# An attention and two gated projections on one core: later conversions, fewer raw tiles in flight, a third v buffer, and no 224-column product

## The chip, the cores and the metric

One NeuronCore of a Trainium2 chip runs the whole kernel. TensorE (PE) multiplies, VectorE (DVE), ScalarE (ACT) and GpSimd (POOL) do the elementwise work, SyncE (SP) issues the DMAs. The metric is the device time of one execution in microseconds (us); lower is better.

## The reference, cut to what matters

```python
# q, k, v: (4, 8, 576, 64); attention with a mask of its own for each half of the heads
scores = scale * np.matmul(q, k.transpose(0, 1, 3, 2))
mask_local   = (rel >= 0) & (rel < 32)                       # heads 0 to 3
mask_strided = (rel >= 0) & (pos_k % 32 == pos_q % 32)       # heads 4 to 7
scores = np.where(masks, scores, -1e9) - max
attn = np.exp(scores); attn = attn / (sum + 1e-9)
x = np.matmul(attn, v)              # then (2304 tokens, 512)
h = x @ w_in;  x = (h * np.cos(h)) @ w_out                   # 512 -> 2048 -> 512
g = x @ w_gate; x = (g * sigmoid(g) * (x @ w_val)) @ w_out2  # 512 -> 1536 -> 512
```

The weights reach the chip as 64-bit floats, and each projection is computed from two f16 halves of each operand, with three products (high by high, high by low, low by high).

## The kernel before, in words

The order of all work is written out by hand; each engine takes its instructions in program order, and SP takes the DMA issues in program order.

**Attention.** A unit is one batch and one pair of heads (16 units), worked in pairs of a strided and a local unit. Each unit has three groups, so 48 groups, alternating strided and local; six groups make a pair of units. The loop over k runs over the groups with lags: at step k come the sums of group k-2, the transposes (PE) of group k-5, the scores of group k (f32 products of 64 by 64, then the mask added by a bf16 product with an identity), the row maxima (DVE), the copy to the output tile `xy` of group k-7 (`put`, ACT), the evacuation of the transposes of k-5 (ACT), the products with v of k-6, the exponentials of k-1 (ACT), then `pump`, then the normalization of k-2 (POOL). `scale_q` (POOL) scales the q of the next pair's units at the third and fourth group of a pair. Line 361, in `scores`, adds a product of 224 columns of ones in an unused part of the bank. PSUM has four banks for scores, and a new one waits until the exponentials of its former user are done. `keep_warm` is a product of 384 columns into a bank of its own; before the change it runs only behind group 47.

**Loads.** `load_qk` brings a unit's q and k (three buffers per kind), `load_v` its v (two buffers per kind: two DMAs for a strided unit, one for a local one). At the last group of a pair the q/k of the third next pair and the v of the next pair are issued. `load_raw` brings one 128 x 512 tile of weights in 64-bit words, in the order of `order`: 16 tiles of w_in, 16 of w_out (scanned for their maxima), again 16 of w_out and so on. `RAW` tiles are in flight; each conversion or scan issues the next.

**Conversions.** A list (`fill`) of small steps with a cost each (about us of DVE) runs beside the main work. `pump(share)` adds `share` to a credit and runs steps while the credit is positive. For w_in a tile costs 1.62: `g0` (ACT, cost 0, line 207, reads the raw tile), `g1`, `g2`, `g3` (DVE, lines 210, 214, 218); the `g0` of the next tile is emitted ahead of the `g1` of this one, and `g3` issues the next raw load. Before w_in's tile `XSAT` + 1 come the maxima and the split of block 0 of the tokens. Then come the splits of w_in into halves, each beside a scan of a w_out tile (1.33 together). `KP` is the first group at which the pump runs, `PUMP` its share.

**Projections.** Behind the attention the first projection runs over five blocks of tokens and 16 tiles of w_in, each with 12 products of 512 columns (lines 465 to 467), then ACT and DVE make the cosine (lines 496 to 507); w_out is converted and used from about the 23rd of these steps on, the other weights later. `need` runs the list up to a wanted step.

Of the kernel before, what the change touches and what calls it, by code (L numbers as in the profile page):

```python
# [10 lines left out]
F32 = mybir.dt.float32  # L11
# [18 lines left out]
LT = S // 64  # L30
LW = 64 + STRIDE
# [6 lines left out]
SP = -(-ST // 2)  # L38
# [9 lines left out]

LAGS = (2, 5, 6, 7)
WARM = 11  # L50
PUMP, KP = 1.0, 5
XSAT = 12
EARLY, K0 = 1, 1
HEAD = 21
RATE, MINLAG = 0.8, 2
RAW = 6
XM = 3
SHARE, SHARE2, SHARE3, SB = 0.95, 0.8, 0.4, 2

# [1 line left out]
def is_local(p):  # L61
    return p < NPAIR // 2
# [6 lines left out]
def build(tc, qk_l, qk_s, v_l, v_s, w_in, w_out, w_gate, w_val, w_out2, mask_l, mask_s, eye32, eye16, out):  # L69
    nc = tc.nc  # L70
    wide = w_in.dtype != F32
    with ExitStack() as ctx:
# [11 lines left out]
        id16 = small.tile([128, 128], BF16, name="id16")  # L84
        ones16 = small.tile([128, 128], BF16, name="ones16")
# [58 lines left out]
        def load_raw():  # L144
            if not order:
                return
            mat, i = order.popleft()
            src = MATS[mat][i]
            if wide:
                t = ring.tile([128, 512, 2], I32, name="raw", bufs=RAW)  # L150
                nc.sync.dma_start(out=t.rearrange("p n w -> p (n w)"), in_=src.bitcast(I32))
            else:
                t = ring.tile([128, 512], F32, name="raw", bufs=RAW)
                nc.sync.dma_start(out=t, in_=src)
            raw.setdefault((mat, i), deque()).append(t)
# [20 lines left out]
        def pump(share):  # L176

            credit[0] = min(credit[0] + share, max(share, 1.0))
            while fill and credit[0] > 0:
                step_fill()  # L180
# [114 lines left out]
        ap = attn.enter_context(tc.tile_pool(name="attn", bufs=2, side="right"))  # L295
        pm = ctx.enter_context(tc.tile_pool(name="pm", bufs=4, space=bass.MemoryType.PSUM))
        pa = attn.enter_context(tc.tile_pool(name="pa", bufs=2, space=bass.MemoryType.PSUM))
        id32 = ap.tile([128, 128], F32, name="id32", bufs=1)
        ml = ap.tile([128, 4, LW], BF16, name="ml", bufs=1)
        ms = ap.tile([128, 4, SW], BF16, name="ms", bufs=1)  # L300
        e_s = [ap.tile([128, 4, 64], F32, name=f"e_s{i}", bufs=1) for i in range(4)]
        e_l = [ap.tile([128, 3, LW + 1], F32, name=f"e_l{i}", bufs=1) for i in range(4)]
        hot = ap.tile([128, 512], BF16, name="hot", bufs=1)
        nc.vector.memset(hot, 1.0)
        v_pair = [ap.tile([128, 2 * SP, 128], F32, name=f"v_pair{i}", bufs=1) for i in range(2)]
        for d in e_s:
            nc.gpsimd.memset(d, 0.0)
            nc.gpsimd.memset(d[:, :, SW:SW + 1], 1e-9)
# [5 lines left out]
        units = [(b, p) for b in range(NB) for p in (2, 0, 3, 1)]  # L314
        qk_t, v_t = {}, {}

        def load_qk(i):
            b, p = units[i]
            loc = is_local(p)
            qk_t[i] = ap.tile([128, QKW[loc]], F32, name="qkl" if loc else "qks", bufs=3)  # L320
            nc.sync.dma_start(out=qk_t[i], in_=(qk_l if loc else qk_s)[b, p % 2])

        def load_v(i):
            b, p = units[i]
            loc = is_local(p)
            if loc:
                v_t[i] = ap.tile([LW, LT, 128], F32, name="vl")
                nc.sync.dma_start(out=v_t[i], in_=v_l[b, p % 2])
            else:
                v_t[i] = v_pair[i // 2 % 2]  # L330
                for u in range(2):
                    nc.sync.dma_start(out=v_t[i][64 * u:64 * u + SW, SP * u:SP * u + SP, :], in_=v_s[b, p % 2, u])

# [7 lines left out]
        class Group:  # L341
# [7 lines left out]
            def scores(self):  # L349
                n, w = self.n, self.w  # L350
                b = bank()
                self.sc = b[:, 0:n * w].rearrange("p (n w) -> p n w", w=w)
                mask = (ml[:, 0:3] if self.g == 0 else ml[:, 1:4]) if self.loc else ms[:, 0:n]
                for i in range(n):
                    q0 = (64 if self.loc else SW) * (self.i0 + i)
                    k0 = (S if self.loc else QP) + q0
                    for h in range(2):
                        r = slice(64 * h, 64 * h + 64)
                        nc.tensor.matmul(out=self.sc[r, i, :], lhsT=qk_t[self.i][r, q0:q0 + 64], rhs=qk_t[self.i][r, k0:k0 + w],  # L359
                                         start=i == 0, stop=False)  # L360
                nc.tensor.matmul(out=b[:, 288:512], lhsT=ones16, rhs=hot[:, 0:224], start=False, stop=False)  # L361
                nc.tensor.matmul(out=self.sc, lhsT=id16, rhs=mask, start=False, stop=True)

            def top(self):
# [188 lines left out]
        gs = [Group(i + d, g) for i in range(0, len(units), 2) for g in range(3) for d in range(2)]  # L553
        load_qk(0)
        load_qk(1)
        for t, a in ((id16, eye16), (ms, mask_s), (ml, mask_l), (id32, eye32)):
            nc.sync.dma_start(out=t, in_=a)
        load_v(0)
        load_v(1)
        load_raw()  # L560
        load_qk(2)
        load_raw()
        load_qk(3)
        load_raw()
        load_v(2)
        load_v(3)
        load_raw()
        load_qk(4)
        load_raw()
        load_qk(5)  # L570
        load_raw()
        warm = bank()
        for _ in range(WARM):
# [14 lines left out]
        def keep_warm():  # L588
            t = bank()[:, 0:4 * LW].rearrange("p (n w) -> p n w", w=LW)
            nc.tensor.matmul(out=t, lhsT=id16, rhs=ml, start=True, stop=True)  # L590

        for k in range(len(gs) + LAGS[3] + 1):
            def group(lag):
                return gs[k - lag] if 0 <= k - lag < len(gs) else None
            i, g = 2 * (k // 6), k % 6
            if group(LAGS[0]):
                group(LAGS[0]).sums()
            if group(LAGS[1]):
                group(LAGS[1]).transposes()
            if group(0):  # L600
                group(0).scores()
                group(0).top()
                if g in (2, 3) and i + g < len(units):
                    scale_q(i + g)
            begun = k - len(gs) - K0
            if 0 <= begun < 2 * EARLY:
                m = begun // 2
                if begun % 2 == 0:
                    need(("in", m))
                    early = up1(0, m, range(KC // 2))  # L610
                else:
                    up1(0, m, range(KC // 2, KC), early)
                    up1_a(early)
                    steps.append((0, m, early))
                    if m:
                        up1_b(steps[-2][2])
            elif not group(0):
                keep_warm()
            if group(LAGS[3]):
                group(LAGS[3]).put()  # L620
            if group(LAGS[1]):
                group(LAGS[1]).evac()
            if group(LAGS[2]):
                group(LAGS[2]).values()
            if group(0) and g == 5:
                for j in (i + 6, i + 7):
                    if j < len(units):
                        load_qk(j)
                for j in (i + 2, i + 3):
                    if i and j < len(units):  # L630
                        load_v(j)
            if group(1):
                group(1).exps()
            pump(PUMP if k >= KP else 0)
            if group(LAGS[0]):
                group(LAGS[0]).norm()

# [213 lines left out]
```

## Time and profile before

| | |
|---|---|
| median of 3 runs | 947.25 us (943.33 to 947.49) |
| profiled execution | 946.87 us, span of its trace 944.9 us |
| PE busy | 909.9 us (96% of the span) |
| DVE busy | 505.2 us (53%) |
| ACT busy | 410.3 us (43%) |
| POOL busy | 130.7 us (14%) |
| mean granted clock of TensorE | 0.98 |
| DMA | 72.12 MB, mean 76 GB/s |

The profiled execution stands 2.0 us above its own span, and 0.4 us below the median. The shares are averages over stages with different limits: the attention takes the first 112 us, the first projection with its cosine the time up to about 520 us, the gated one the rest.

### The profile page before, as it was taken

To read this page: it belongs to the slowest core of one execution; us is meant where nothing else is said; L and a number is where in the kernel's file an instruction comes from. 1 tells how busy PE (TensorE), PEld (TensorE's weight loads), DVE (VectorE), ACT (ScalarE), POOL (GpSimd) and SP (SyncE) were. 2 spreads that over 40 slices of the span, in tenths; PEclk is the share of its full clock that TensorE was granted. 3 is DMA by queue.
4 is the path that set the end of the run, shared out by engine and by line. 5 is a ranking of instruction groups with operands and counts; after the bars stand their busy time and mean duration, and the time that the engine had idled before them with its cause. 6 is when DMAs were issued, how large, how long until landed. Compare 5 with 4: busy or idle time off the path is not lost.

```text
span 944.9 us, 14190 instructions
## 1 busy us (share of the span) xinstructions
PE 909.9 (96%) x5608; PEld 474.5 (50%) x5608; DVE 505.2 (53%) x1012; ACT 410.3 (43%) x845; POOL 130.7 (14%) x175
## 2 busy tenths in 40 slices
PE   7999978799999998999999999999999999999998
PEld 4667633344444443444577544444444444444587
DVE  4599877879833557693375663333233322332333
ACT  4689977765432445754465432222112211221222
POOL 3244223221121021222222000000000000000000
PEclk7599999999999999999999999999999999999999
DMA  9998841246400222051000200010001000100010
GB/s 305 309 298 256 261 132 45 89 136 192 142 0 23 90 90 67 1 222 45 23 23 24 67 1 1 1 44 1 1 1 45 1 1 0 45 1 1 8 38 23
DMA packets 21554, 72.12 MB, mean 76 GB/s; under 512 B 2704, under 2 KB 3472, under 8 KB 21488
## 3 DMA queue, kind: packets, MB, share of 16 engines
q1 hardware_dynamic: 21488, 71.22, 23.6%
q8 instruction: 44, 0.72, 0.3%
q14 instruction: 22, 0.18, 0.1%
HBM read 66.49 MB, written 4.72 MB: 75 GB/s over the span
## 4 chain that ended last, share of the span: by engine, by line
PE 80%; DVE 9%; ACT 6%; issue 3%; POOL 1%; DMA 1%; SPq 0%; ACTq 0%; DVEq 0%; POOLq 0%
PE bank L465 13%; PE bank L466 13%; PE bank L467 13%; PE acc L466 10%; PE acc L467 10%; PE acc L465 10%; PE bank L359 3%; PE po L412 3%; DVE tb L505 1%; PE tp L390 1%; DVE cv L218 1%; DVE tb L499 1%; PE bank L361 1%; PE tp L394 1%; ACT wo L228 1%
## 5 line engine op out<-in xcount | busy, mean ns | idle before, releaser
L465 PE MATMUL bank<-xs,spare 128*128 128x512 f16 (+1 forms) x480 | 171.9, 358 | 0.3 <-DVE ta L535 0.3
L466 PE MATMUL bank<-xs,spare 128*128 128x512 f16 (+1 forms) x480 | 171.9, 358 | 0.0
L467 PE MATMUL bank<-xs,spare 128*128 128x512 f16 (+1 forms) x480 | 171.9, 358 | 0.0
L465 PE MATMUL bank<-xs,wi 128*128 128x512 f16 (+1 forms) x320 | 115.9, 362 | 19.0 <-DVE tb L505 15.3
L535 DVE SCALAR_TENSOR_TENSOR ta<-ta,bank 128x512 f32<-128x512 f32 (+1 forms) x60 | 38.1, 635 | 168.9 <-ACT ta L534 168.9
L466 PE MATMUL bank<-xs,wi 128*128 128x512 f16 (+1 forms) x320 | 116.0, 362 | 0.0
L467 PE MATMUL bank<-xs,wi 128*128 128x512 f16 (+1 forms) x320 | 115.8, 362 | 0.0
L534 ACT ACTIVATE ta<-bank,c 128x512 f32<-128x512 f32 (+1 forms) x60 | 38.6, 643 | 168.6 <-PE bank L467 168.6
L466 PEld LDWEIGHTS <-wi 128*128 128x128 f16 x560 | 54.9, 98 | 76.4 <-issue 25.1
L537 ACT ACTIVATE g<-ta 128x512 f16<-128x512 f32 (+1 forms) x60 | 35.3, 588 | 132.5 <-DVE ta L536 132.5
L496 ACT ACTIVATE tb<-bank,quarter,c 128x512 int32<-128x512 f32 (+1 forms) x80 | 58.3, 729 | 70.2 <-PE bank L467 54.1
L466 PE MATMUL acc<-g,wi 128*128 128x512 f16 (+1 forms) x240 | 85.9, 358 | 0.9 <-DVE g L538 0.6
L465 PE MATMUL acc<-g,wi 128*128 128x512 f16 (+1 forms) x240 | 85.9, 358 | 0.4 <-ACT g L537 0.4
L467 PE MATMUL acc<-g,wi 128*128 128x512 f16 (+1 forms) x240 | 86.0, 358 | 0.0
L465 PEld LDWEIGHTS <-wi 128*128 128x128 f16 x560 | 55.0, 98 | 59.7 <-issue 6.3
L467 PEld LDWEIGHTS <-wi 128*128 128x128 f16 x560 | 55.0, 98 | 56.8 <-issue 3.8
L507 POOL TENSOR_TENSOR g<-tb,g 128x512 f16<-128x512 f32 (+1 forms) x48 | 50.8, 1059 | 186.7 <-ACT g L506 163.1
L466 PEld LDWEIGHTS <-spare 128*128 128x128 f16 x480 | 46.9, 98 | 46.8 <-issue 0.6
L465 PEld LDWEIGHTS <-spare 128*128 128x128 f16 x480 | 46.9, 98 | 46.5
L467 PEld LDWEIGHTS <-spare 128*128 128x128 f16 x480 | 46.9, 98 | 46.5
L501 ACT ACTIVATE tb<-tb,right 128x512 f32<-128x512 f32 (+1 forms) x80 | 53.9, 674 | 36.7 <-DVE tb L499 36.2
L467 PE MATMUL acc<-g,wo 128*128 128x512 f16 (+1 forms) x192 | 66.0, 344 | 0.0
(122 smaller groups left out, 1445.5 us busy)
## 6 DMA issues: line engine op xcount, KB each, us to landing
raw<-w_out SPq DMA_DIRECT2D x56, 512.0 KB, 5.3
raw<-w_in SPq DMA_DIRECT2D x16, 512.0 KB
raw<-w_gate SPq DMA_DIRECT2D x12, 512.0 KB, 3.8
raw<-w_val SPq DMA_DIRECT2D x12, 512.0 KB, 4.6
qks<-qk_s SPq DMA_DIRECT2D x8, 594.0 KB, 5.2
qkl<-qk_l SPq DMA_DIRECT2D x8, 592.0 KB, 8.6
out<-xy SPq DMA_DIRECT2D x16, 256.0 KB, 2.3
vl<-v_l SPq DMA_DIRECT2D x8, 432.0 KB, 6.7
```

What stands on the lines that cost most here:

```text
L218: nc.vector.scalar_tensor_tensor(out=u, in0=box["l"], scalar=29, in1=u, op0=ALU.logical_shift_right, op1=ALU.bitwise_or)
L359: nc.tensor.matmul(out=self.sc[r, i, :], lhsT=qk_t[self.i][r, q0:q0 + 64], rhs=qk_t[self.i][r, k0:k0 + w], start=i == 0, stop=False)
L412: nc.tensor.matmul(out=self.po[64 * h:64 * h + 64, i * qn:i * qn + qn], lhsT=v_t[self.i][0:r, t, 64 * h:64 * h + 64], rhs=pt[:, 64 * h:64 ...
L465: nc.tensor.matmul(out=o, lhsT=w[:, 0, c], rhs=x[0], start=first, stop=False)
L466: nc.tensor.matmul(out=o, lhsT=w[:, 0, c], rhs=x[1], start=False, stop=False)
L467: nc.tensor.matmul(out=o, lhsT=w[:, 1, c], rhs=x[0], start=False, stop=last)
L496: nc.scalar.activation(out=c["w"].bitcast(I32), in_=c["ph"], func=AF.Identity, scale=turn[c["blk"]], bias=quarter)
L501: nc.scalar.activation(out=c["w"], in_=c["w"], func=AF.Sin, scale=TWO_PI, bias=right)
L507: nc.gpsimd.tensor_tensor(out=g[:, 1, 0:n], in0=w, in1=g[:, 0, 0:n], op=ALU.subtract)
L534: nc.scalar.activation(out=t, in_=pg, func=AF.Tanh, scale=half[blk])
L535: nc.vector.scalar_tensor_tensor(out=t, in0=t, scalar=1.0, in1=pg, op0=ALU.add, op1=ALU.mult)
L537: nc.scalar.activation(out=g[:, 0, 0:n], in_=t, func=AF.Copy)
```

## The change

The pump starts at group 7 instead of 5 and adds 0.85 instead of 1.0; the scaling of block 0 comes after tile 10 instead of 12. Three raw tiles are loaded at the start, a fourth is added at group 24, and there are four buffers instead of six. v has three buffers of each kind, and its loads move from the last group of a pair to the first of the next. The first loads come in another order: q/k 0 and 1, the masks and the bf16 identity, q/k 2 and 3, the f32 identity, v 0 to 3, then raw tiles between q/k 4 and 5. The 224-column product of each group is taken out, and `keep_warm` runs at groups 3 to 8.

```diff
-PUMP, KP = 1.0, 5
-XSAT = 12
+PUMP, KP = 0.85, 7
+XSAT = 10
-RAW = 6
+RAW = 4
...
-        v_pair = [ap.tile([128, 2 * SP, 128], F32, name=f"v_pair{i}", bufs=1) for i in range(2)]
+        v_pair = [ap.tile([128, 2 * SP, 128], F32, name=f"v_pair{i}", bufs=1) for i in range(3)]
...
-                v_t[i] = ap.tile([LW, LT, 128], F32, name="vl")
+                v_t[i] = ap.tile([LW, LT, 128], F32, name="vl", bufs=3)
...
-                v_t[i] = v_pair[i // 2 % 2]
+                v_t[i] = v_pair[i // 2 % 3]
...
-                nc.tensor.matmul(out=b[:, 288:512], lhsT=ones16, rhs=hot[:, 0:224], start=False, stop=False)
...
-        for t, a in ((id16, eye16), (ms, mask_s), (ml, mask_l), (id32, eye32)):
+        for t, a in ((ms, mask_s), (ml, mask_l), (id16, eye16)):
             nc.sync.dma_start(out=t, in_=a)
-        load_v(0)
-        load_v(1)
-        load_raw()
         load_qk(2)
-        load_raw()
         load_qk(3)
-        load_raw()
-        load_v(2)
-        load_v(3)
+        nc.sync.dma_start(out=id32, in_=eye32)
+        for i in range(4):
+            load_v(i)
         load_raw()
         load_qk(4)
+        load_qk(5)
         load_raw()
-        load_qk(5)
         load_raw()
...
+            if 3 <= k < 9:
+                keep_warm()
...
+            if group(0) and g == 0:
+                for j in (i + 2, i + 3):
+                    if i and j < len(units):
+                        load_v(j)
             if group(0) and g == 5:
                 for j in (i + 6, i + 7):
                     if j < len(units):
                         load_qk(j)
-                for j in (i + 2, i + 3):
-                    if i and j < len(units):
-                        load_v(j)
...
             pump(PUMP if k >= KP else 0)
+            if k == len(gs) // 2:
+                load_raw()
```

## Rows read from the trace of the kernel before

**Rows 1.** The page's head and slices: the span in 40 equal parts of 23.6 us. Digits are busy tenths, PEclk is the granted clock in tenths of full speed, GB/s what the DMA engines moved.

```profile
span 944.9 us, 14190 instructions
PE   7999978799999998999999999999999999999998
PEclk7599999999999999999999999999999999999999
DMA  9998841246400222051000200010001000100010
GB/s 305 309 298 256 261 132 45 89 136 192 142 0 23 90 90 67 1 222 45 23 23 24 67 1 1 1 44 1 1 1 45 1 1 0 45 1 1 8 38 23
```

**Rows 2.** Windows by stage: from and to, length, busy time (and instructions) of PE, PE's weight loads, DVE, ACT and POOL, then the granted clock, the DMA engines' share, GB/s.

```profile
0.00:106.00 106.00, 99.79 (x1392) 68.67 (x1394) 80.43 (x226) 79.27 (x292) 39.01 (x82) 0.86 0.91 288
112.00:260.00 148.00, 131.59 (x640) 59.27 (x639) 119.25 (x208) 99.66 (x162) 34.87 (x33) 0.99 0.42 129
600.00:700.00 100.00, 100.00 (x465) 45.24 (x463) 32.56 (x52) 20.93 (x33) 0.00 (x0) 1.00 0.03 11
```

**Rows 3.** The chain of waits in order of time, 0 to 300 us, of it the score products of groups 7, 13, 15, 17 and 47 (local groups, 12 products each): start, length, what.

```profile
21.47 1.15 PE bank L359 x12
...
40.53 1.15 PE bank L359 x12
...
45.91 0.64 PE bank L359 x12
49.45 0.64 PE bank L359 x12
...
105.95 0.64 PE bank L359 x12
```

**Rows 4.** The timeline from 10 to 19 us: start, length, engine, line, operation, out<-in, count, and in brackets the idle time before it and what ended it. The first four lines are groups 4, 0 and 2; the last is the scores of group 6.

```profile
10.24 0.43 PEld L359 LDWEIGHTS bank<-qks 64*64 64x64 f32 x12 [0.21 <-ACT e_s L373]
10.84 0.23 PE L362 MATMUL bank<-ms,id 128*128 128x162 bf16 x1
10.88 0.17 DVE L382 RECIPROCAL ls<-ls 128x4 f32<-128x4 f32 x1
11.05 0.90 ACT L373 ACTIVATE e_s<-bank,mx 128x54 f32<-128x54 f32 x4 [0.19 <-DVE ls L382]
13.36 0.69 POOL L339 TENSOR_SCALAR qks<-qks 128x594 f32<-128x594 f32 x1 [6.57 <-DMA qks<-qk_s]
14.01 0.55 POOL L383 TENSOR_TENSOR e_s<-e_s,ls 128x216 f32<-128x216 f32 x1
14.61 0.29 PEld L394 LDWEIGHTS tp<-id,e_s 128*128 128x128 f32 x2 [3.77 <-POOL e_s L383]
18.23 1.10 PE L359 MATMUL bank<-qks 64*64 64x54 f32 x16
```

**Rows 5.** Windows of 0.1 and 0.2 us around the fall and the rise of the granted clock (third number from the end).

```profile
13.20:13.40 0.20, 0.00 (x0) 0.00 (x0) 0.00 (x1) 0.00 (x0) 0.04 (x1) 1.00 1.04 419
13.40:13.60 0.20, 0.00 (x0) 0.00 (x0) 0.00 (x0) 0.00 (x0) 0.20 (x1) 0.67 1.10 435
...
44.00:44.10 0.10, 0.10 (x6) 0.10 (x6) 0.00 (x1) 0.10 (x1) 0.10 (x1) 0.50 0.79 179
44.20:44.40 0.20, 0.20 (x12) 0.20 (x11) 0.00 (x0) 0.20 (x2) 0.20 (x1) 1.00 0.86 228
```

**Rows 6.** The timeline of PE: the 224-column product (L361) and the product behind it (L362) at the low and at the full clock, and two keep-warm products (L590) with what follows them.

```profile
35.10 0.37 PE L361 MATMUL bank<-hot,ones 128*128 128x224 bf16 x1
35.27 0.45 PE L362 MATMUL bank<-ml,id 128*128 128x288 bf16 x1
...
84.21 0.27 PE L361 MATMUL bank<-hot,ones 128*128 128x224 bf16 x1
84.32 0.29 PE L362 MATMUL bank<-ml,id 128*128 128x288 bf16 x1
...
116.43 0.50 PE L590 MATMUL bank<-ml,id 128*128 128x384 bf16 x2
116.76 0.38 PE L465 MATMUL bank<-xs,wi 128*128 128x512 f16 x1
```

**Rows 7.** Windows of 10 us, columns as in rows 2.

```profile
0.00:10.00 10.00, 8.35 (x74) 4.18 (x75) 4.26 (x8) 2.01 (x5) 3.34 (x24) 1.00 0.81 250
10.00:20.00 10.00, 6.03 (x58) 3.68 (x59) 5.27 (x17) 6.21 (x22) 3.64 (x6) 0.67 1.03 341
20.00:30.00 10.00, 10.00 (x105) 6.93 (x105) 5.11 (x15) 6.08 (x22) 3.07 (x6) 0.50 1.02 389
...
90.00:100.00 10.00, 10.00 (x169) 7.13 (x168) 9.39 (x30) 9.71 (x38) 4.83 (x8) 1.00 0.73 241
```

**Rows 8.** DMA issues: out<-in, engine, operation, count, size of one, median us from issue to landing where the trace has it.

```profile
raw<-w_in SPq DMA_DIRECT2D x16, 512.0 KB
...
qks<-qk_s SPq DMA_DIRECT2D x8, 594.0 KB, 5.2
...
vl<-v_l SPq DMA_DIRECT2D x8, 432.0 KB, 6.7
v_pair<-v_s SPq DMA_DIRECT2D x16, 162.0 KB
```

**Rows 9.** Waits, who for whom: us in total, times, the longest. The first is of all engines from 112 to 260 us (the same total stands for 0 to 260), the second of SP's queue from 0 to 130 us.

```profile
PE bank L465 <- DVE tb L505: 15.3, 9, 4.8
...
SPq L151 <- DVE wi L218: 40.2, 12, 7.5
```

**Rows 10.** The timeline from 16 to 19 us: the first conversion of a raw tile, its four instructions (the ACT line holds those of two tiles).

```profile
16.18 1.24 ACT L207 ACTIVATE wi<-raw 128x512 f32<-128x512 f32 x2
...
17.41 0.68 DVE L210 TENSOR_REDUCE pw_in<-raw 128x1 f32<-128x512 f32 x1
18.00 0.42 DVE L214 TENSOR_SCALAR wi<-wi 128x512 int32<-128x512 int32 x1
18.45 0.69 DVE L218 SCALAR_TENSOR_TENSOR wi<-raw,wi 128x512 int32<-128x512 int32 x1
```

**Rows 11.** The timeline of PE at 157 us, in the first projection.

```profile
157.08 0.38 PE L465 MATMUL bank<-xs,wi 128*128 128x512 f16 x1 [1.81 <-DVE tb L505]
```

## Prediction

> **What bounds the kernel now.** I read the page's slices first. TensorE (PE) is at 9 tenths of nearly every slice, so whatever moves the end must move PE; but its granted clock is 0.5 in the second slice, and the DMA engines are at 8 or 9 tenths through the first four slices and idle later [rows 1]. Then the windows by stage. The attention (0 to 106 us) has PE busy 99.8 of 106 us at a mean clock of 0.86 and the DMA at 0.91. From 112 to 260 us PE is busy only 131.6 of 148 us; later it is full [rows 2]. All that the diff touches lies in the first 112 us, with an echo up to 260 us. So the sum goes over when the attention ends, and over whether the stage behind it waits more.
>
> Then the chain of waits in order of time. The scores of group 7 start at 21.47, of group 13 at 40.53, of group 15 at 45.91, of group 17 at 49.45, of group 47 at 105.95 us [rows 3]. From 7 to 13 a group takes 19.06 / 6 = 3.18 us, from 17 to 47 it takes 56.5 / 30 = 1.883 us. The narrow windows say why: the granted clock falls to 0.5 (1.2 GHz) at 13.5 us and is back at 1.0 (2.4 GHz) at 44.2 us [rows 5], although PE had no gap for most of that time. What PE did before the fall stands in the timeline: its next weight load stood at 14.61 after 3.77 us of waiting for GpSimd (POOL), whose normalization of group 0 started at 14.01. Its operand was ready at 11.05, but ahead of it in POOL's queue stood the scaling of the third q/k tile, which waited 6.57 us for a DMA, up to 13.36 [rows 4]. So a late load stops POOL, POOL stops PE, PE loses its clock, and nine groups (6 to 14) run at 3.18 us.
>
> **The change part by part.** *New order of loads.* The q/k tiles 2 and 3 are now issued ahead of all v and raw tiles. A q/k tile is 594 KB (0.61 MB), a v pair 162 x 2 + 432 KB (0.77 MB), a raw tile 512 KB (0.52 MB) [rows 8]; masks and identities are 0.25 MB by their shapes. The queue moved 250 GB/s in the first 10 us, 341 in the next, 389 in the third [rows 7]: 2.5 MB by 10 us, 5.9 by 20, 9.8 by 30. In the order of before tile 2 ends at 3.37 MB, which this rate puts at 12.6 us, and it landed at 13.36: about 0.8 us is to be added. In the new order it ends at 2.0 MB, so it lands by 9 us. Then group 0 is normalized at 11.05 to 11.6 us, and its transposes go at about 12.8 instead of 14.61. In between, the new keep-warm products each take one of the four PSUM banks, so the scores of groups 3 and 4 wait for ScalarE's (ACT) exponentials of groups 0 and 2, which end at 10.2 and 11.95 [rows 4]: two gaps of about 1 us where now there is one of 3.5. From the transposes on PE goes through, and group 6 has its scores at about 14.5 instead of 18.23 us [rows 4]: -3.7 us. The six products of 384 columns cost 0.17 us each (116.43 to 116.76 for two, [rows 6]); four lie in gaps, the last two cost 0.3 us. I take it that the clock stays at 1.0 over this place.
>
> *The 224-column product.* From its start to the start of the next product is 0.11 us at 2.4 GHz (84.21 to 84.32) and 0.17 at 1.2 GHz (35.10 to 35.27) [rows 6]; I take 0.105 for the fast one, since the times are rounded. A fast group then takes 1.883 - 0.105 = 1.78 us. For that to be gained, VectorE (DVE) and ACT must keep up: they are busy 9.39 and 9.71 of 10 us in 90 to 100 [rows 7], 1.77 and 1.83 us of a group. The pump of 0.85 takes 0.15 of a unit of conversion away, by the first conversion (0.68 + 0.42 + 0.69 us of DVE and 0.62 of ACT for 1.62 units, [rows 10]) 0.17 us of DVE and 0.06 of ACT: 1.60 and 1.77 us. It just fits; if ACT is what binds, the gain is 0.07 instead of 0.105 us a group.
>
> *Nine groups at the fast clock:* 9 x (3.18 - 1.78) = -12.6 us. *The 33 groups from 15 on:* 33 x 0.105 = -3.5 us. With the start, -19.8 us.
>
> *Fewer raw tiles in flight, loaded later.* This is the price. In the order of the new list raw tile 0 ends at 4.75 MB, tile 1 at 6.49 MB, and tile 3, which stands behind q/k 6 and 7 and v 4 and 5, at 9.53 MB: at the rates above 16.6, 21.5 and 29.3 us, landing at about 17.4, 22.3 and 30.1. The pump starts at group 7, whose turn is at about 17 us, and its first call emits the ACT conversions of tiles 0 and 1 together, as at 16.18 now [rows 10]. Tile 3 is asked for at group 10. Taking ACT to work in order, as POOL did in [rows 4], evacuations and exponentials stand behind a conversion whose tile is not there. PE can go on for about 1.3 groups (2.3 us). That gives: ACT blocked from 17.9 to 22.3, PE idle some 2.4 us before group 10; ACT blocked from 28 to 30.1, PE idle some 2.9 us at group 12, nothing having been regained in between; then at the q/k and v loads of groups 11 and 17 bursts of 1.2 + 0.77 MB, 5.7 us at 0.35 MB/us (between the rates of [rows 7]), against a lead of two units (3.8 groups or 6.7 us) less up to one unit: some 2 us each. Sum +9.3 us. The bounds: 0, if PE's lead absorbs all of it, and 16, if every block reaches PE whole. After group 24 a fourth tile is in flight and the q/k loads end at group 29, so nothing is charged there. Now six tiles give a lead of four units (about 12 us), and neither ACT nor PE waits for a raw tile at all; it is SP that waits, 40.2 us for the buffers [rows 9].
>
> The Trainium skill, "TensorE: Matmul & The Clock Gate", its paragraph on engine queue depths, says that ACT and DVE work strictly first in, first out; only PE pulls weight loads forward. By that rule the +9.3 us stand; if ACT could go round a conversion that waits, they would be 0. The trace shows the rule for POOL (normalization behind scaling, [rows 4]) and not for ACT, which waits for no DMA in it.
>
> *The third buffer for v* and its loads at the first group of a pair instead of the last: three DMA issues a pair, five groups earlier, moved past the raw loads of those groups on SP's queue. No engine waits for v now, so 0; it makes the burst above come in one piece, which is in its price.
>
> *Pump and start.* Before, 51 pumps of 1.0; after, 49 of 0.85 = 41.65: 9.35 units, about 10 us of DVE work, move behind the attention, where PE loses 15.3 us to DVE already [rows 9]. Block 0 asks for one split (1.33 units with its scan) in a slot that pumps 1.28, with five done ahead, and the second product starts only some 23 slots later; so no one is forced to wait. Bounds 0 and +5 us; I take 1. XSAT moves the scaling of block 0 from group 24 to about 26, after its last input at group 18: 0.
>
> Sum: -19.8 + 0.3 + 9.3 + 1 = -9.2 us. The profiled execution took 946.87 us (span 944.9 and 2.0 around it), 0.4 below the median of 947.25. So 946.9 - 9.2 = 937.7, said as 938.
>
> **The rivals.** *A, forecast:* the clock stays up, ACT's waits eat half of the gain. With the bounds of the two prices: 928 to 949, its own likely range 930 to 946.
>
> *B, the clock falls once and comes back.* The idle of about 2.4 us before group 10 is as long as the one after which the clock fell now (PE's last work ended at 11.07, the fall is at 13.5, [rows 4, 5]). If it falls at 24 us and stays low as long as now, 30.7 us, ten groups cost 3.18 - 0.16 = 3.02 instead of 1.78 us: +12.8. The loads catch up meanwhile, so the waits shrink to some 4.4 us: -19.8 + 0.3 + 2.4 + 12.8 + 2 + 1 = -1.3, or 945.5 (941 to 950). For it: the waits as worked out. Against it: 1.8 us of idle before 157.08 left the clock alone, but with dense products around it [rows 11].
>
> *C, other side: the clock falls and does not come back in the attention.* Its one recovery in this stream took 30 us of gapless work with the 224-column product in every group; without it nothing in the rows shows that it recovers before the dense products behind group 48. From group 10 at 24.1 us, 38 groups at 3.02 us end at 139 instead of 107.8: +31, or 978. It decides as soon as one of ACT's waits lasts long enough; if all raw tiles land 2 us earlier than I have them, it does not happen.
>
> *D, no stall at all:* the raw tiles come in time, ACT and PE run through: 946.9 - 19.8 + 1.3 = 928. Against it: 24 groups at that pace have asked for twelve q/k, ten v and eleven raw tiles by 47 us, some 17 MB or 0.37 MB/us without a pause, when the first four slices moved 0.26 to 0.31 [rows 1].
>
> **The numbers.** A with D 0.46 (D alone 0.06), B 0.23, C 0.26, and 0.05 for several falls and rises (950 to 965). Half a per cent, 4.7 us, is about what a measurement of this kernel can tell from no change. Faster than 942.2: six sevenths of A and D, a fifth of B, 0.45. Within: some of A, most of B, 0.19. Slower: 0.36. The range reaches from 930 to 980, leaving out D's end and the worst of C.
>
> **What would show it.** Right: clock 1.0 from 6.6 us through the attention; the transposes of group 0 by 13 us; ACT waiting for raw tiles near 18 to 22 and 28 to 30 us; a group at 1.78 us after group 24; group 47's scores at 95 to 98 us instead of 105.95. Wrong: a clock of 0.5 behind the first ACT wait (B, C), no ACT wait on a DMA (D), or PE idle above 20 us between 112 and 260 us instead of 16.4.

## The result and the profile after

The changed kernel is slower: a median of 960.3 us (953.9 to 979.1, four runs) against 946.2 (943.3 to 947.5, four runs), a ratio of 1.0116 with a 95% interval of 1.0071 to 1.0161. The forecast was 938. All ratios here leave out executions that stand more than 1.5% above the fastest of their kernel; medians and ranges hold all of them. The profiled execution took 956.9 us, 10.0 above the one of before.

The record also gives the mean granted clock of every execution. Since the clock stands at 1.0 or at 0.5, twice the share that is missing to 1, times the span, estimates for how long it was low: 69 us in the profiled execution (68 by its trace), and 55, 83 and 127 us in the other three. For the executions of the kernel before that stand beside the experiments the same estimate is 17 to 65 us.

The page's head and slices after, 23.9 us each; the rows of before are [rows 1].

```profile
span 955.1 us, 14116 instructions
...
PE   7899997898999998999999999999999999999998
...
PEclk9559998999899999999999999999999999999999
DMA  9968553235630233033010120010001000100010
GB/s 304 266 189 246 166 177 89 67 113 181 193 110 1 67 92 107 1 119 146 1 45 24 45 66 1 1 45 1 1 1 44 1 1 1 45 1 1 1 45 23
```

The first slice has gained: clock digit 9 instead of 7. The second and third have a 5, where before only the second had one. The windows say where and how long (columns as in [rows 2]): first around the fall and the rise of the granted clock, then 30 us at the low clock, then a table of 10 us, then the two stages.

```profile
23.40:23.50 0.10, 0.00 (x0) 0.00 (x0) 0.00 (x0) 0.00 (x0) 0.00 (x0) 0.99 1.40 558
23.50:23.60 0.10, 0.00 (x0) 0.00 (x0) 0.00 (x0) 0.00 (x0) 0.00 (x0) 0.50 0.83 340
71.20:71.30 0.10, 0.10 (x2) 0.00 (x0) 0.04 (x1) 0.00 (x0) 0.10 (x1) 0.57 0.23 95
71.30:71.40 0.10, 0.10 (x3) 0.02 (x2) 0.00 (x0) 0.00 (x0) 0.10 (x1) 1.00 0.93 332
...
40.00:70.00 30.00, 30.00 (x304) 21.66 (x305) 16.48 (x47) 19.06 (x68) 8.57 (x14) 0.50 0.65 201
...
10.00:20.00 10.00, 9.57 (x148) 6.58 (x146) 5.05 (x18) 6.18 (x26) 3.45 (x6) 1.00 1.03 270
20.00:30.00 10.00, 4.70 (x49) 3.54 (x51) 6.35 (x18) 5.60 (x20) 3.62 (x5) 0.67 1.02 332
30.00:40.00 10.00, 7.16 (x74) 4.95 (x70) 3.55 (x10) 4.37 (x19) 1.67 (x3) 0.50 1.02 283
...
0.00:106.00 106.00, 95.08 (x1232) 67.21 (x1234) 68.40 (x190) 69.94 (x259) 37.05 (x78) 0.77 0.79 240
112.00:260.00 148.00, 133.26 (x679) 60.27 (x679) 116.72 (x215) 102.01 (x178) 35.78 (x34) 0.94 0.45 137
```

From 10 to 20 us PE is now busy 9.57 us at the full clock, where it was 6.03 at 0.67 [rows 7]: the early stall is gone. But at 23.5 us the clock falls to 1.2 GHz, and comes back only at 71.3: 47.8 us, where before it was low for 30.7 (13.5 to 44.2, [rows 5]). In between stand 30 us without any gap of PE at 0.50. What PE did before the fall stands in the timeline (start, length, engine, line, operation, out<-in, count, idle time before and what ended it); of the lines behind 361, those cited here are now one lower than in [rows 4], since line 361 is gone. The last three lines are of the stage behind the attention.

```profile
11.62 0.44 PE L393 MATMUL tp<-id,e_s 128*128 128x128 f32 x2 [0.30 <-POOL e_s L382]
13.35 0.67 PE L359 MATMUL bank<-qks 64*64 64x54 f32 x16
...
19.77 0.67 ACT L207 ACTIVATE wi<-raw 128x512 f32<-128x512 f32 x1 [3.25 <-DMA raw<-w_in]
24.00 0.66 ACT L207 ACTIVATE wi<-raw 128x512 f32<-128x512 f32 x1 [3.56 <-DMA raw<-w_in]
25.30 0.91 PE L411 MATMUL po<-pt,vl 96*64 96x64 f32 x12 [5.37 <-ACT pt L400]
35.63 0.66 ACT L207 ACTIVATE wi<-raw 128x512 f32<-128x512 f32 x1 [6.46 <-DMA raw<-w_in]
36.85 1.11 PE L411 MATMUL po<-pts,v_pair 118*64 118x54 f32 x16 [2.84 <-ACT pts L400]
...
157.48 0.61 PE L466 MATMUL bank<-xs,wi 128*128 128x512 f16 x1 [3.01 <-DVE wi L231]
180.80 0.59 PE L464 MATMUL bank<-xs,wi 128*128 128x512 f16 x1 [3.20 <-DVE tb L504]
240.29 0.59 PE L464 MATMUL bank<-xs,wi 128*128 128x512 f16 x1 [4.60 <-DVE tb L504]
```

The transposes of group 0 start at 11.62 instead of 14.61, the scores of group 6 at 13.35 instead of 18.23 [rows 4]. Then ACT, the engine of the evacuations, stands three times before a conversion whose raw tile has not landed (3.25, 3.56, 6.46 us), and PE stands behind ACT for 5.37 and 2.84 us. The clock falls inside the first of these. The scores of groups 13, 15, 17 and 47 in the chain of waits after, against 40.53, 45.91, 49.45 and 105.95 [rows 3]:

```profile
38.58 1.15 PE bank L359 x12
44.72 1.15 PE bank L359 x12
...
50.39 1.15 PE bank L359 x12
...
112.96 0.64 PE bank L359 x12
```

For the account I take the start of each group's mask product, before and after. Group 9: 29.2 and 19.6, so 9.6 us ahead. Group 24: 63.2 and 72.0, so 8.8 behind. Of those 18.4 us, 5.4 and 2.8 are PE's two stalls, before group 10 and before group 13; the remaining 10.2 stand in the longer time at the low clock. Group 47: 106.6 and 113.5, 6.9 behind. In the stage behind the attention I count the products at the first of its three product lines (465 before, 464 after), from 0 on; "product 160" comes at 237.7 and 248.0, 10.2 behind, and from there on nothing changes: the first product of the gated stage starts at 514.2 and 524.5, and the spans differ by 10.3.

### The profile page after: what moved, and what is told of

It reads as the page before. It is cut to its first block, busy times and chain, and to the rows that moved or that the text cites. A ratio compares the mean times of both kernels' runs of the same rounds, so it can differ in the third digit from the quotient of the medians.

```text
span 955.1 us, 14116 instructions
## 1 busy us (share of the span) xinstructions
PE 917.1 (96%) x5566; PEld 479.8 (50%) x5566; DVE 505.6 (53%) x1013; ACT 411.6 (43%) x845; POOL 131.0 (14%) x175
## 4 chain that ended last, share of the span: by engine, by line
PE 82%; DVE 8%; ACT 4%; DMA 3%; issue 2%; ACTq 0%; DVEq 0%
PE bank L464 14%; PE bank L466 14%; PE bank L465 14%; PE acc L465 10%; PE acc L466 10%; PE acc L464 10%; PE bank L359 3%; PE po L411 3%; DMA raw<-w_in 1%; DMA qkl<-qk_l 1%; DVE cv L218 1%; DVE tb L504 1%; PE tp L389 1%; DVE tb L498 1%; PE bank L361 1%
## 5 line engine op out<-in xcount | busy, mean ns | idle before, releaser
L464 PE MATMUL bank<-xs,wi 128*128 128x512 f16 (+1 forms) x320 | 118.1, 369 | 12.8 <-DVE tb L504 8.2
L466 PE MATMUL bank<-xs,wi 128*128 128x512 f16 (+1 forms) x320 | 117.7, 368 | 4.5 <-DVE wi L231 4.4
L465 PE MATMUL bank<-xs,wi 128*128 128x512 f16 (+1 forms) x320 | 117.7, 368 | 0.0
L465 PEld LDWEIGHTS <-spare 128*128 128x128 f16 x480 | 47.0, 98 | 46.7 <-issue 0.6
```

Of the source, the lines that this page charges most:

```text
L464: nc.tensor.matmul(out=o, lhsT=w[:, 0, c], rhs=x[0], start=first, stop=False)
L465: nc.tensor.matmul(out=o, lhsT=w[:, 0, c], rhs=x[1], start=False, stop=False)
L466: nc.tensor.matmul(out=o, lhsT=w[:, 1, c], rhs=x[0], start=False, stop=last)
```

## The experiments

Each diff is against the changed kernel unless it says "before". Group times are starts of mask products, as above.

**The product put back.**

```diff
+                nc.tensor.matmul(out=b[:, 288:512], lhsT=ones16, rhs=hot[:, 0:224], start=False, stop=False)
```

> The changed kernel with the 224-column product put back into every group, all else as changed. Theory P (the product decides how long the low clock lasts): ACT's waits for raw tiles stay (up to about 24 and 36 us), the clock falls at about 23.5 us as in the changed kernel, but is back some 30 us later, near 55 us, instead of 47.8 us later; group 47 has its scores at about 109 to 111 us instead of 113.5, and the time is 950 to 957 us. Rival Q (the product has no part in the recovery): the low stretch stays near 48 us and the product costs 14 x 0.16 + 24 x 0.105 = 4.8 us on top: 960 to 968 us.

Measured: 948.9 us (946.0 to 951.6, ten runs), ratio 1.0013 (0.998 to 1.0046), an interval that does not touch that of the changed kernel. The timeline and a window:

```profile
21.14 0.67 ACT L207 ACTIVATE wi<-raw 128x512 f32<-128x512 f32 x1 [4.56 <-DMA raw<-w_in]
27.01 0.91 PE L412 MATMUL po<-pt,vl 96*64 96x64 f32 x12 [6.73 <-ACT pt L401]
...
24.00:46.00 22.00, 17.56 (x175) 12.16 (x177) 10.80 (x30) 12.85 (x48) 5.54 (x10) 0.50 0.93 272
```

The stall is the same, even longer (6.73 us), and the clock falls at the same place (22.9 us). But it is back at 46.8, after 23.9 us instead of 47.8. So the product does not keep the clock up. Where the stall stands, the way back is shorter with it, and that is worth more than its 0.1 us in each group: the time is below even the 950 to 957 us of theory P. By the mean clocks this holds for all ten executions: low for 25 to 44 us in each, against 55 to 127 us in the changed kernel.

**The product taken from the kernel before**, and nothing else.

```diff
-                nc.tensor.matmul(out=b[:, 288:512], lhsT=ones16, rhs=hot[:, 0:224], start=False, stop=False)
```

> The kernel before with only the 224-column product taken out. Theory P: the clock falls at 13.5 us as before and comes back clearly later than 44.2 us, or not before the dense products behind group 48; each further 10 us of it cost 3.3 groups x 1.24 = 4 us, so 950 to 985 us. Rival Q: the clock is back near 44 us and the product's own time is gained: 947 - 9 x 0.16 - 33 x 0.105 = 942 us.

Measured: 941.8 to 987.0 us, median 961.4; ratio 0.9979 (0.9933 to 1.0025). Half of the ten executions stand at 972 to 987, where none of 25 of the kernel before was above 958.4. In the profiled one (943.5) the clock was low from 13.8 to 30.9 and again from 71.9 to 75.3 us, behind two waits of PE for v:

```profile
69.48 0.33 PE L411 MATMUL po<-pts,v_pair 118*64 118x54 f32 x4 [1.13 <-DMA v_pair<-v_s]
70.86 0.56 PE L411 MATMUL po<-pts,v_pair 118*64 118x54 f32 x12 [1.06 <-DMA v_pair<-v_s]
...
31.00:68.00 37.00, 35.96 (x616) 26.92 (x615) 35.20 (x102) 33.82 (x129) 16.56 (x26) 1.00 1.01 319
```

Without the product the clock can come back as well (here after 17 us) and stays up while the stream runs (31 to 68 us). By the mean clocks, the clock was low for some 109 to 148 us in the five executions from 972 us up, and for 30 to 47 us in the other five. Where and why no profile shows, so nothing is built on them; in the others the product is worth nothing that can be measured, and neither theory is settled by this kernel.

**The pump settings alone**, in the kernel before.

```diff
-PUMP, KP = 1.0, 5
-XSAT = 12
+PUMP, KP = 0.85, 7
+XSAT = 10
```

> The kernel before with only the pump of the change: KP 7, PUMP 0.85, XSAT 10. Loads, buffers and the 224-column product as before. Theory D (deferred conversions cost): the attention ends as before (scores of group 47 at 105 to 107 us), but in the first projection PE waits more, some 3 to 6 us between 112 and 260 us: 949 to 954 us. The prediction's own step: nothing is forced, 0 to +1: 946 to 948 us.

Measured: 944.3 us (941.4 to 961.3), ratio 0.9958 (0.9918 to 0.9997), the fastest by its ratio. In the profiled execution (941.7) the clock was low from 15.1 to 25.4 us only, and group 47 came at 99.2 instead of 106.6. By the mean clocks this is one of the two with the least time at the low clock (24 us; the ten lie between 24 and 75), so that gain is not put down to the pump. From group 47 to product 160 it took 133.5 instead of 131.1 us. So in these two profiles the deferral costs 2.4 us, with no other part of the change present.

**The conversions much later.** Group 16 instead of 7, the fourth tile at group 9.

```diff
-PUMP, KP = 0.85, 7
+PUMP, KP = 0.85, 16
...
-            if k == len(gs) // 2:
+            if k == 9:
```

> The changed kernel with the pump from group 16 instead of 7, and its fourth raw tile loaded at group 9 instead of 24, so that the first conversions find their tiles in place. Theory W (ACT's waits are what drops the clock): ACT waits for raw tiles less than 2 us in all, the clock stays at 1.0 from 6.4 us through the attention without the 224-column product, and group 47 has its scores at 88 to 92 us instead of 113.5. 9 more pumps (7.65 units) move behind the attention, so the total is 935 to 948 us. Rival: the stream without the product cannot hold the clock, which falls anyway before 60 us; group 47 stays above 100 us and the total above 955.

Measured: 977.3 us (968.5 to 994.3), ratio 1.0211 (1.0121 to 1.0302). Theory W had said 935 to 948. The timeline and windows of the profiled execution (985.4):

```profile
49.55 0.66 ACT L207 ACTIVATE wi<-raw 128x512 f32<-128x512 f32 x1 [7.27 <-DMA raw<-w_in]
50.85 0.91 PE L411 MATMUL po<-pt,vl 96*64 96x64 f32 x12 [5.62 <-ACT pt L400]
...
10.00:20.00 10.00, 9.64 (x159) 7.00 (x158) 6.22 (x23) 8.73 (x36) 4.12 (x7) 1.00 1.02 269
20.00:30.00 10.00, 9.22 (x162) 6.88 (x158) 4.59 (x18) 7.65 (x31) 5.55 (x10) 1.00 1.03 341
30.00:40.00 10.00, 9.98 (x167) 7.23 (x165) 7.80 (x23) 9.67 (x38) 3.48 (x6) 1.00 1.01 275
...
60.00:90.00 30.00, 30.00 (x306) 21.68 (x306) 16.55 (x47) 17.72 (x63) 7.93 (x13) 0.50 0.63 199
```

Two things in one trace. Up to 48.9 us the stream runs at 2.4 GHz without the product, (34.14 - 27.17) / 4 = 1.74 us a group from 13 to 17, so it needs no such product as long as it isn't stopped. But the DMA share is 1.0 from 10 to 40 us, and the wait that ended at 19.8 us now ends at 49.6 and is longer. It is for the fifth raw tile. The first four were in place; the load of the fifth could be issued only at 36.6 us, when the first conversion had freed one of the four buffers, and took some 13 us to land in the full queue. Behind it the clock was low to 137.7 us in this execution, 88.8 us, past the end of the attention: the picture of rival C.

**Six raw tiles, all loaded at the start**, with the product left out and with it, and with padded v.

```diff
-PUMP, KP = 0.85, 7
+PUMP, KP = 0.85, 9
...
-RAW = 4
+RAW = 6
...
-        for i in range(4):
-            load_v(i)
+        load_v(0)
+        load_v(1)
         load_raw()
-        load_qk(4)
-        load_qk(5)
         load_raw()
+        load_qk(4)
         load_raw()
+        load_qk(5)
+        load_v(2)
+        load_v(3)
+        for _ in range(3):
+            load_raw()
...
-            if k == len(gs) // 2:
-                load_raw()
```

> The changed kernel with the raw tiles undone: six buffers, all six loaded at the start (two ahead of q/k 4, one between q/k 4 and 5, three behind v 3), the pump from group 9; no 224-column product, three v buffers as changed. Theory W (ACT's waits for raw tiles drop the clock, nothing else in the change does): ACT waits less than 3 us for raw tiles in all, the clock holds at 1.0 through the attention, group 47 has its scores at 92 to 98 us instead of 113.5, and the time is 932 to 942 us. Rival V (the DMA engines are full, so the wait moves to another load): q/k or v tiles come late instead, PE idles more than 2 us somewhere before 60 us, the clock falls and stays low for 20 us or more, 950 to 985 us.

> As e5_raw6_early, with the 224-column product in every group. If the clock holds in both, the product only costs: 42 x 0.1 = 4 us more than e5_raw6_early. If there are stalls that drop the clock, the product bounds what they cost: the runs lie close together (as in e1_after_with_224, 946 to 952) while those of e5_raw6_early scatter; 936 to 946 us.

Measured: 971.2 us (948.6 to 976.7, four runs) without the product, too scattered for a ratio; 952.3 (946.8 to 956.0) with it, ratio 1.0054 (1.0021 to 1.0087). First the timeline without the product, then that with it:

```profile
34.09 0.69 POOL L339 TENSOR_SCALAR qks<-qks 128x594 f32<-128x594 f32 x1 [4.73 <-DMA qks<-qk_s]
```

```profile
51.84 0.66 ACT L207 ACTIVATE wi<-raw 128x512 f32<-128x512 f32 x1 [6.59 <-DMA raw<-w_in]
53.19 0.90 PE L412 MATMUL po<-pts,v_pair 118*64 118x54 f32 x12 [6.20 <-ACT pts L401]
```

The first is above the 932 to 942 of theory W, the second above its 936 to 946. More tiles early only make another load late: once q/k (the clock falls at 36.9 us and is back at 112.0), once a raw tile (it falls at 51.2 and is back at 64.9). Then v was padded, so that each of its strided halves is loaded into 64 partitions instead of 54, to ask whether that transfer's shape makes the queue slow; with the product, then without it.

```diff
-                    nc.sync.dma_start(out=v_t[i][64 * u:64 * u + SW, SP * u:SP * u + SP, :], in_=v_s[b, p % 2, u])
+                    nc.sync.dma_start(out=v_t[i][64 * u:64 * u + 64, SP * u:SP * u + SP, :], in_=v_s[b, p % 2, u])
```

> As e6_raw6_with_224, with each strided v half loaded as 64 partitions (ten of them zeros from the host's layout) instead of 54, two DMAs as before. If the slow v transfers (250 to 280 GB/s beside 400 for q/k and raw tiles) come from an uneven share of the DMA engines, the windows with v reach 330 GB/s or more, the waits left in e6 shrink, and it is 1 to 4 us faster than e6. Rival: the rate stays, the time is that of e6, since 18% more bytes move for these tiles.

> As e7_raw6_224_padv without the 224-column product. Theory W: with the fewest waits of all, the clock holds and this is the fastest kernel, 928 to 938 us. Rival: one stall of 2 us or more in the attention is enough, and the runs scatter up to 980 us.

Measured: 952.6 us (947.8 to 955.9), ratio 1.0054 (1.0024 to 1.0084), as without padding; and 958.8 (952.4 to 978.8), ratio 1.0136 (1.0065 to 1.0207). ACT waits 5.99 and 5.94 us for a raw tile near 49 and 52 us. With the product, the window from 30 to 40 us moves 277 GB/s instead of 241 (part of it the zeros of the padding), but no wait goes and the time is the same. Without it the two sets of four runs lie too far apart to tell.

**No later v loads.** Units 4 to 15 use the v tiles of units 0 to 3: that part of the computation is left out.

```diff
+            if i >= 4:
+                v_t[i] = v_t[i % 4]
+                return
```

> The changed kernel without the v loads of units 4 to 15 (these units reuse the v tiles of units 0 to 3, which leaves that part of the computation out): 4.6 MB less to load in the attention, every engine instruction as changed. Theory F (the DMA engines are full up to 70 us, and that is what makes ACT wait): the first two waits of ACT (raw 0 and 1, before 24 us) stay, since the loads ahead of them stay, but the third (6.5 us, to 35.6) shrinks below 3 us, no later wait appears, and the attention ends earlier: group 47 at 98 to 108 us if the clock still falls at 23.5 us. Rival G (too few raw buffers, the DMA has room): the third wait stays near 6 us although there are fewer bytes.

Measured: 951.7 us (942.2 to 977.1), ratio 1.0000 (0.9957 to 1.0044). The stall of PE, the third wait of ACT, and windows (the last two around the rise of the clock):

```profile
26.29 0.91 PE L414 MATMUL po<-pt,vl 96*64 96x64 f32 x12 [6.53 <-ACT pt L403]
30.39 0.66 ACT L207 ACTIVATE wi<-raw 128x512 f32<-128x512 f32 x1 [0.22 <-DMA raw<-w_in]
...
30.00:40.00 10.00, 10.00 (x98) 7.03 (x99) 6.18 (x18) 6.20 (x24) 1.70 (x4) 0.50 0.63 230
30.00:60.00 30.00, 30.00 (x307) 21.68 (x307) 16.73 (x47) 18.90 (x67) 7.86 (x13) 0.50 0.53 179
63.70:63.80 0.10, 0.10 (x1) 0.00 (x0) 0.10 (x2) 0.00 (x0) 0.00 (x0) 0.78 0.00 0
63.80:63.90 0.10, 0.10 (x3) 0.09 (x4) 0.10 (x3) 0.00 (x0) 0.00 (x0) 1.00 0.00 0
```

With fewer bytes the third wait is 0.22 us instead of 6.46, and the DMA share from 30 to 40 us falls from 1.02 to 0.63. This is the one edit that took a wait away instead of moving it, and by the ratio the time is that of the kernel before, with an interval that does not touch that of the changed kernel. The first two waits (4.45 and 3.50 us) stay, since the first loads are the same, and the clock still falls, at 22.8 us. The trace settles one more thing. In the changed kernel a second stall of PE (2.84 us, up to 36.85) stands inside the low stretch and might be what keeps the clock down. Here PE has no second gap, and without the 224-column product the clock is low for 41.0 us all the same, up to 63.7, against 23.9 with it.

**A slow pump first.** The order of loads of the six-tile kernel, four tiles at the start, one more at groups 18 and 21, conversions at half pace up to group 24; without the product and with it.

```diff
-            pump(PUMP if k >= KP else 0)
-            if k == len(gs) // 2:
+            pump((0.5 if k < 24 else 1.0) if k >= KP else 0)
+            if k in (18, 21):
                 load_raw()
```

> As e5_raw6_early (six raw buffers, early q/k, three v buffers, no 224-column product) but with the demand for raw tiles halved while the DMA is full: the pump adds 0.5 from group 9 to 23 and 1.0 from group 24, four raw tiles at the start and one more at groups 18 and 21. Theory F: no wait above 2 us for a DMA in the attention, the clock holds at 1.0 without the product, group 47 at 92 to 97 us, time 930 to 940 us. Rival: the DMA is late for q/k or v even so, the clock falls, and the runs scatter from 945 to 985 us.

> As e10_slow_pump with the 224-column product in every group. If the clock holds in both, it is 3 to 5 us slower than e10_slow_pump: 935 to 944 us. If it falls in e10_slow_pump, this one lies between 938 and 948 us with little scatter.

Measured: 972.7 us (959.9 to 981.5), ratio 1.0157 (1.0058 to 1.0257), and 955.0 (953.0 to 961.3), ratio 1.0085 (1.0051 to 1.0118). Both miss what I hoped for, 930 to 940 and at most 948. ACT still waits, later, in the first (timeline):

```profile
49.70 0.66 ACT L207 ACTIVATE wi<-raw 128x512 f32<-128x512 f32 x1 [5.50 <-DMA raw<-w_in]
51.01 0.91 PE L411 MATMUL po<-pt,vl 96*64 96x64 f32 x12 [4.86 <-ACT pt L400]
```

With the product group 47 comes at 98.8 us, 7.9 earlier than before, and yet the kernel is slower: product 160 comes at 244.5 instead of 237.7. What the attention no longer converts, the projection behind it waits for: there PE waits longest in total for DVE at line 231, the splits of w_in (10.4 us; before, none of this kind), and the clock falls more often.

**The product in the first 24 groups only**: first in the kernel before with the changed pump settings, then in the changed kernel.

```diff
+                if self.i < 8:
+                    nc.tensor.matmul(out=b[:, 288:512], lhsT=ones16, rhs=hot[:, 0:224], start=False, stop=False)
```

> The kernel before with the changed pump settings (start at group 7, 0.85, scaling of block 0 after tile 10), and with the 224-column product in the first 24 groups only. Theory P (the product pays only while the clock is low, and the low stretch lies in the first half): the low stretch begins near 15 us and lasts 10 to 24 us, and groups 24 to 47 go at 1.78 to 1.81 us instead of 1.90, so 2 us less than with the product everywhere: a median of 941 to 943 us and a highest time not above 962. Rival Q (a late wait for v near 70 to 75 us also drops the clock in some executions, and without the product it stays low): single times of 965 to 985 us among the ten, and a median of 944 to 955. Rival R (ScalarE sets the pace of the second half, not TensorE): groups 24 to 47 still at 1.88 to 1.90 us, and a median of 943.5 to 945.

> The changed kernel with the 224-column product put back in the first 24 groups only. Theory P: the low stretch begins at 23 us and ends between 44 and 55 us, as with the product everywhere, and groups 24 to 47 go at 1.81 us: a median of 945 to 949 us, 12 to 15 below the changed kernel. Rival Q (what the product does for the clock, it does in the second half too): a low stretch behind group 24, single times over 960 us, and a median of 950 to 962.

Measured: 945.3 us (939.6 to 964.3), ratio 0.9977 (0.9948 to 1.0007), above the 941 to 943 of theory P; and 946.9 (944.5 to 953.8), ratio 1.001 (0.9987 to 1.0033), inside its 945 to 949. The second, timeline and windows:

```profile
27.19 0.91 PE L413 MATMUL po<-pt,vl 96*64 96x64 f32 x12 [7.00 <-ACT pt L402]
...
46.60:46.70 0.10, 0.10 (x6) 0.08 (x2) 0.00 (x0) 0.10 (x2) 0.02 (x1) 0.53 0.41 164
46.70:46.80 0.10, 0.10 (x4) 0.00 (x0) 0.00 (x0) 0.10 (x2) 0.00 (x0) 1.00 0.79 246
...
75.00:105.00 30.00, 30.00 (x521) 22.56 (x522) 27.79 (x80) 28.82 (x111) 12.70 (x20) 1.00 0.64 183
```

The clock falls at 22.8 and is back at 46.7 us, as with the product everywhere, and behind group 24 a group takes (105.4 - 63.4) / 23 = 1.83 us instead of 1.90. So where PE has been stopped the product pays, and where the clock is already up it costs 0.07 us a group in the trace; the times of the two kernels (ratios 1.001 and 1.0013) do not tell them apart. By the mean clocks the clock is low for 26 to 51 us in all twelve executions, which lie within 9.3 us. The first kernel has the same quick second half ((102.2 - 60.5) / 23 = 1.81) but a low stretch of 23.9 us in its profiled execution, where the pump settings alone had 10.2; it is not faster than with those alone. No version beat the kernel before by more than the 0.5% that a measurement of it can tell.

## Why the prediction was wrong

**The start** was right in its mechanism, its size too small: the early stall went, group 6 came 4.9 us earlier (said: 3.7), and PE had no gap of a microsecond up to group 9.

**Fewer raw tiles in flight** was right in kind, and its sum came out near by luck. ACT's waits were said at 17.9 to 22.3 and 28 to 30.1 us; there were three, which ended at 19.8, 24.0 and 35.6. PE's two stalls were 5.37 and 2.84 us against 2.4 and 2.9, and the two later waits of 2 us each did not come (PE has no gap of a microsecond from 36.9 us to the end of the attention). So 8.2 us of stalls against 9.3 charged hide a first stall of more than twice its size. The conversions began 2.4, 1.7 and 5.5 us later than the landings worked out. The mis-sized term is the rate: I took the MB per us of the old order of loads [rows 7], 341 and 389 GB/s from 10 to 30 us, and the changed order moved 270 and 332 at the same share of 1.0. What sets the rate was not found. (The v loads stand five groups earlier than before, at the first group of the same pair, as the prediction has it, and not of the next pair.) The forecast had no row for ACT keeping its order. Now there is one: ACT stands 6.46 us at line 207, and the evacuation at line 400 that PE waits for comes behind it. With that the trace agrees with the Trainium skill, "TensorE: Matmul & The Clock Gate", paragraph on engine queue depths, which calls ACT strictly first in, first out.

**The step that failed** is "A, forecast: the clock stays up". The sum charged the stall before group 10 with its own length, 2.4 us, and put its effect on the clock at nothing, although the text itself, under B, calls it as long as the idle time in which the clock had fallen. The runs showed a stall of 5.37 us, a fall of the clock inside it, and 47.8 us at the low clock; besides the 8.2 us of the stalls themselves, that put group 24 another 10.2 us behind. The size of the stall may have had its part in it: in this execution the clock fell 3.6 us after PE's last work (19.93 to 23.50), later than a stall of 2.4 us would have lasted. That a shorter stall would have left the clock up is not shown; in the kernel before without the product two gaps of 1.1 us stood ahead of a fall.

B had the place (said 24, was 23.5 us), but took the length from before, 30.7 us with the product in every group, for a stream that no longer had the product. Its +12.8 for ten groups is also a slip: 10 x 1.24 = 12.4. Put into B, 47.8 us are four to six more groups at the slow rate, 5 to 7 us; stalls of 8.2 instead of 4.4 are 3.8, the stage behind the attention 2.4 more than charged, the start 1.2 less. That makes 10 to 12 of the 11.4 us between its 945.5 and 956.9. C priced the same loss to the end of the attention. So the gain of nine groups at the fast clock, -12.6, was not lost but spent: the groups 6 to 9 were fast, and 10 to 23 slow in their place.

The trace of before held one more sign that the text did not use. Against B it names an idle time of 1.8 us before 157.08 that left the clock alone [rows 11]. In the same stage stands a longer one, in which the clock fell (timeline, then a window):

```profile
140.01 0.58 PE L465 MATMUL bank<-xs,wi 128*128 128x512 f16 x1 [4.83 <-DVE tb L505]
...
139.80:143.10 3.30, 3.09 (x8) 1.14 (x8) 1.37 (x6) 1.46 (x3) 1.16 (x1) 0.50 0.27 104
```

It fell at 139.8 and was back at 143.2 us, behind eight products of 512 columns.

**The 224-column product** was taken as work that only costs. Group 24 to 47 went at (113.53 - 71.99) / 23 = 1.81 us; with 1.89 before, measured in the same way, that is a gain of 0.08 a group, nearer to ACT's bound (0.07) than to the 0.105 taken. Against these 2 us stand some 10 us by the two ratios with and without it in the changed kernel (1.0013 and 1.0116). Its second effect, on the length of a low stretch, was seen under C ("nothing in the rows shows that it recovers") and got no part in the forecast.

**Pump and start**: +1 was said, bounds 0 and +5. From group 47 to product 160, kernels with the old pump settings took 131.1 and 131.3 us, with the new ones 132.6 to 135.1: +1.3 to +4. What was missed there is the clock: PE idles less between 112 and 260 us than before (14.7 us against 16.4, so my sign for a costly deferral did not show), but the clock is 0.94 instead of 0.99. Three of the gaps after, 3.01, 3.20 and 4.60 us long, have a fall of the clock in them, and it is low for 17.1 us in that stage; before it was one gap (4.83 us) and 3.4 us.

**What stays open.** The length of a low stretch in the attention without the product ran from 3 to 89 us over the profiled executions; with it, from 10 to 31. In the changed kernel the causal step is shown by two edits that bring the product back (in every group, and in the first 24), with intervals that do not touch its own. In the pairs with other load orders the intervals of the ratios overlap (or there is none). By the mean clocks they point the same way: low for 21 to 48 us in the 29 executions with the product, and for 34 to 119 us, all but two above 50, in the 12 without. In the kernel before the ratio shows no difference. What lifts the clock in this stream isn't known: from 40 to 70 us PE had no gap, and the clock stayed at 0.50.

## What to carry to other kernels

Price a stall of TensorE with what its clock does afterwards: here 5.4 us of idle cost another 10 us in the groups behind it. Where a queue is full (a DMA share of 1.0), moving a load earlier or its user later moved the wait to another load here; only the edit with fewer bytes removed one. Before removing work that looks idle, ask what it does in the disturbed part of the run, and if it does something there, keep it there. (That removing it elsewhere pays is seen in the trace, 0.07 us a group, and not in the times.)

## What the runs showed of the hardware

A gapless stream of small f32 products and transposes can stay at 1.2 GHz for tens of microseconds (30.00 of 30 us busy at 0.50 after; the same again in the kernel with late conversions), though the same stream holds 2.4 GHz when it enters at that level. One bf16 product of 224 columns in each group, some 0.1 of 1.9 us, halved the low stretch in the profiled executions of the changed kernel (47.8 to 23.9 us). In the stage of f16 products of 512 columns (112 to 260 us, before and after) the four low stretches lasted 3.4 to 6.8 us.

At a DMA share of about 1.0 the queue moved 269 to 389 GB/s in the windows of 10 us shown here. The pace of PE does not sort them: 341 and 389 beside a stopped or slow PE [rows 7], but 283 beside a slow one in the kernel after (30 to 40 us), and in the kernel before 349 beside a PE at the full clock:

```profile
60.00:70.00 10.00, 9.67 (x167) 6.99 (x163) 9.15 (x27) 8.44 (x35) 4.71 (x8) 1.00 1.02 349
```

The orders of loads differ too, so the cause is not told apart.
